# A transformer block on one core: transposing the second LayerNorm and b1 on TensorE, a shorter query ring for a fourth ffn1 weight slot, and an earlier second output projection

## The chip, the core and the metric

The kernel runs on one core of a Trainium2 chip. The core has five engines with a queue each: TensorE (PE; its weight loads are shown as PEld), VectorE (DVE), ScalarE (ACT), GpSimd (POOL) and SyncE (SP), which here issues every DMA. An engine takes its instructions in order; a wait at the head of its queue holds everything behind it. The metric is the device time of one execution in microseconds (us). Lower is better.

## What is computed

A pre-LayerNorm transformer block over 2048 tokens of width 1024, in bf16: attention with 32 heads of 32, then a feed-forward layer of width 3584 with tanh GELU, each added to its input.

```python
def _A_ref(x, wqkv, wo):                    # H = 32, Dh = 32
    qkv = (x @ wqkv).reshape(B, S, 3, H, Dh).transpose(2, 0, 3, 1, 4)
    q, k, v = qkv[0], qkv[1], qkv[2]
    p = _softmax(jnp.einsum("bhqd,bhkd->bhqk", q, k) * Dh ** -0.5, axis=-1)
    o = jnp.einsum("bhqk,bhkd->bhqd", p, v)
    return o.transpose(0, 2, 1, 3).reshape(B, S, D) @ wo

def _B_ref(x, w1, b1, w2, b2):
    return jnp.einsum("bsf,fd->bsd", _gelu(jnp.einsum("bsd,df->bsf", x, w1) + b1), w2) + b2

h  = x + _A_ref(_layernorm(x), A_wqkv, A_wo)
h2 = h + _B_ref(_layernorm(h), B_w1, B_b1, B_w2, B_b2)
```

## The kernel before

**How the order comes about.** The program does not write its instruction streams out by hand. It builds a graph of tasks (`gr.add`, line 87), each with an engine, an assumed duration, a priority and the buffers it reads and writes, and then `schedule` (line 112) simulates the five engines with these assumed durations and fixes the order of each engine's queue. `assign` (line 209) turns the dependences into semaphore waits. On the chip the order is fixed: where a DMA lands later than the planner assumed (`dma_lat=2.0` and 260 GB/s), the engine waits in place. For PE, `pick_pe` (line 1007) takes score matmuls first, then the value matmuls, then "background" groups in the order in which they were made; a group that isn't ready may be passed by a later one that is. PSUM has eight banks: six hold scores, and the remaining two are shared by one attention accumulator and the background groups, so a background group keeps a bank from its first matmul until DVE has copied it out.

**Stages.** In the lead (lines 857 to 888) x arrives in 16 tiles of 128 tokens; each is normalised by DVE and transposed (four tiles on PE with a copy by ACT, twelve by DMA transposes) into `xnT`, and the first group of four heads gets its keys, queries and values. Then attention goes by jobs `(g, c)`: eight groups g of four heads, eight chunks c of 256 queries, eight rounds a job. A round is 8 score matmuls (L682), two exponentials on ACT of 128x1024 (L690), a sum of two key blocks on DVE (`PS`, L695), 8 value matmuls (L700) and 4 matmuls with ones for the denominator (L719). The first two chunks of each group run while later groups are projected (line 933).

Behind the attention of chunk c run, as background groups, the output projection of chunk c-1 (`wo`, line 767, four groups; result plus x into `hch`), the second LayerNorm (`ln2`, line 781, two tiles of 128 tokens), `ffn1` of chunk c-1 (14 blocks of 256 columns) and `ffn2` of chunk c-2 (four groups `F2` of 29 matmuls). `PLAN` (line 952) gives how the four ffn2 groups and the ffn1 blocks alternate. GELU (line 811) is done for every two ffn1 blocks: square and polynomial on DVE into `a_sq`, tanh on ACT into `a_th`, product on DVE. After the last attention comes the tail (line 974): wo, LayerNorm, ffn1 and ffn2 of the last chunk with nothing beside them, and the tail's LayerNorm is transposed on PE with a copy by ACT.

**What the change touches.**
- `ln2_tile` (line 773): LayerNorm of one tile into the single slot of `R1.xb`, then with "dma" one DMA transpose (`dma_t`, line 522) into `hnT`. The other branch makes a background group of eight PE transposes of 128x128 (`transposes`, line 571) with one copy of the bank to `hnT` by ACT or DVE.
- b1 (lines 912 and 914): 3584 biases loaded so that partition p holds the elements p, p+128, ..., and cast to float by DVE at the lowest priority. They are read first by ffn1 (L804).
- Queries: chunks 0 and 1 are projected right into `QT`; chunks 2 to 7 are projected after the last group (`spill_q`, line 643, 24 groups), written to HBM by way of `stg`, and read back by `load_q` (line 650), eight jobs ahead, into a ring of eight slots.
- `w1r`: three slots of 512 KB for the weights of wo and ffn1 (`R1.w1`); `w2r`: seven for ffn2. In the tail both rings get slots in the space of K and V.
- `layer_norm` has a branch `on_act` that no call takes (`ACT_LN` is empty).

Of the kernel before, what the change touches and what calls it, by code (L numbers as in the profile page):

```python
# [7 lines left out]
ACT = mybir.ActivationFunctionType  # L8
ALU = mybir.AluOpType
# [3 lines left out]
P = 128  # L13
# [299 lines left out]
def build_kernel(nc, A_x, A_wqkv, A_wo, B_w1, B_b1, B_w2, B_b2, out):  # L313
# [47 lines left out]
    ones32, B_ones = sb(top, "ones32", [P, 32], BF)  # L361
    two_row, B_two = sb(top, "two_row", [P, P], BF)
    b2t, B_b2t = sb(top, "b2t", [P, D], BF)
    b1b, B_b1b = sb(top, "b1b", [P, FC], BF)
    b1f, B_b1f = sb(top, "b1f", [P, FC], F32)
    cexp, B_cexp = sb(top, "cexp", [P, 16], F32)
    NLN = 8
# [4 lines left out]
    tb, B_tb = sb(top, "tb", [P, NLN, 1], BF, NLN)  # L372
    denb, B_denb = sb(top, "denb", [P, NLN, 1], BF, NLN)
    rden, B_rden = sb(top, "rden", [P, NLN, 1], F32, NLN)
    nmr, B_nmr = sb(top, "nmr", [P, NLN, 1], F32, NLN)

    kt_lo = top.cur
    KT, B_KT_ = sb(top, "KT", [P, G, S], BF, 8 * G)
# [1 line left out]
    v_lo = top.cur  # L380
    V, B_V_ = sb(top, "V", [P, G, NT, P], BF, 8 * G)
    B_V = [B_V_[8 * g:8 * g + 8] for g in range(G)]
    NQ = 8
    QT, B_QT = sb(top, "QT", [P, NQ, 256], BF, NQ)
    pt_lo = top.cur
    NPT = 7
# [34 lines left out]
    def ring(area, name, n, width, dtype):  # L421
        h, b = sb(area, name, [P, n, width], dtype, n)
        if n == 1:
            b = [b]
        return [(h[:, i, :], b[i]) for i in range(n)]
# [2 lines left out]
        pass  # L428

    R1 = Set()  # L430
    NW1, NW2 = 3, 7
    w1r, B_w1r = sb(ffn, "w1r", [P, NW1, 2048], BF, NW1)
    hch, B_hch_ = sb(ffn, "hch", [P, 2, 2, D], BF, 8)
    B_hch = [B_hch_[:4], B_hch_[4:]]
# [2 lines left out]
    R1.xb = Ring(ring(Area(x_lo), "xb2", 1, D, BF))  # L437
    LN2_PRIO = -2
    hnT, B_hnT = sb(ffn, "hnT", [P, 2, DC, P], BF, 2)
    R1.sq = Ring(ring(ffn, "a_sq", 2, 1024, BF))  # L440
    th_lo = ffn.cur
    R1.th = Ring(ring(ffn, "a_th", 1, 1024, F32))
    stg = Ring(ring(Area(th_lo), "stg", 2, 512, BF))
    R1.os = Ring(ring(ffn, "a_os", 2, 512, BF))
    gT, B_gT_ = sb(ffn, "gT", [P, 2, FC, 256], BF, 2 * FC)
    B_gT = [B_gT_[:FC], B_gT_[FC:]]
# [13 lines left out]
    def c_dve_ps(n):  # L460
        return (120 + n) / 960.0 + 0.02
# [73 lines left out]

    cnt = {"ln": 0}

    def layer_norm(tiles, prio, on_act=False):
        n = len(tiles)
        while cnt["ln"] % NLN + n > NLN:  # L540
            cnt["ln"] += 1
        i = cnt["ln"] % NLN
        cnt["ln"] += n
        for k, (x_ap, B_x, o_ap, B_o) in enumerate(tiles):
            for c in range(2):
                dve(lambda v, c=c, k=k, x_ap=x_ap: v.bn_stats(st_l[:, i + k, 6 * c:6 * c + 6], x_ap[:, 512 * c:512 * c + 512]),  # L546
                    0.68, reads=[B_x[c % len(B_x)]], writes=[B_stl[i + k]], prio=prio)
            dve(lambda v, k=k: v.bn_aggr(mv_l[:, i + k, :], st_l[:, i + k, :]), 0.2,
                reads=[B_stl[i + k]], writes=[B_mv[i + k]], prio=prio)
        sl = slice(i, i + n)  # L550
        dve(lambda v: v.tensor_copy(mvb[:, sl, :], mv_l[:, sl, :]), 0.12, reads=B_mv[sl], writes=B_mvb[sl], prio=prio)
        dve(lambda v: v.tensor_scalar(tb[:, sl, :], mvb[:, sl, 1:2], EPS_BF, None, ALU.add), 0.12,
            reads=B_mvb[sl], writes=B_tb[sl], prio=prio)
        pool(lambda g: g.tensor_tensor(denb[:, sl, 0], tb[:, sl, 0], cexp[:, 0:n], ALU.pow), 0.42 + 0.157 * n,
             reads=B_tb[sl] + [B_cexp], writes=B_denb[sl], prio=prio)
        dve(lambda v: v.tensor_copy(mvr[:, sl, :], mvb[:, sl, 0:1]), 0.12, reads=B_mvb[sl], writes=B_mvr[sl], prio=prio)
        dve(lambda v: v.reciprocal(rden[:, sl, :], denb[:, sl, :]), 0.12, reads=B_denb[sl], writes=B_rden[sl], prio=prio)
        if on_act:
            dve(lambda v: v.scalar_tensor_tensor(nmr[:, sl, :], mvr[:, sl, :], -1.0, rden[:, sl, :], ALU.mult, ALU.mult), 0.12,
                reads=B_mvr[sl] + B_rden[sl], writes=B_nmr[sl], prio=prio)  # L560
        for k, (x_ap, B_x, o_ap, B_o) in enumerate(tiles):
            if on_act:
                act(lambda a, k=k, x_ap=x_ap, o_ap=o_ap: a.activation(
                    o_ap, x_ap, ACT.Identity, bias=nmr[:, i + k, :], scale=rden[:, i + k, :]), 1024,
                    reads=B_x + [B_nmr[i + k], B_rden[i + k]], writes=[B_o], prio=prio, ap_bias=True)
                continue
            dve(lambda e, k=k, x_ap=x_ap, o_ap=o_ap: e.tensor_scalar(
                o_ap, x_ap, mvr[:, i + k, :], rden[:, i + k, :], ALU.subtract, ALU.mult), 0.58,
                reads=B_x + [B_mvr[i + k], B_rden[i + k]], writes=[B_o], prio=prio)
# [25 lines left out]
    def x_slot(tt):  # L595
        return xrb[:, tt % NXR, :], [B_xrb[tt % NXR]]

    def x_tile(tt, prio):
        ap, b = x_slot(tt)
        return dma(ap, x2[tt * P:(tt + 1) * P, :], P * D * 2, writes=b, prio=prio)  # L600

    def ln_tiles(tts, prio, on_act=False):
        layer_norm([x_slot(tt) + (xb[:, tt % NXB, :], B_xb[tt % NXB]) for tt in tts], prio, on_act)

    def tr_tile(tt, evac):
        if evac != "dma":
# [31 lines left out]
                 [grp.buf], [B_V[2 * q][tt // 2], B_V[2 * q + 1][tt // 2]])  # L638

    def slot_of(g, c):  # L640
        return (2 * g + c) % 8 if c < 2 else g

    def spill_q(g, h):
        grp = group(f"s{g}.{h}")
# [136 lines left out]
    def ln2(R, c, evac):  # L781
        for t in range(2):
            ln2_tile(R, c, t, evac)
# [64 lines left out]
    def mixed(R, c1, c2, plan):  # L848
        blk = 0
        for p in plan:  # L850
# [3 lines left out]
            else:  # L854
                ffn2(R, c2, *p)

    x_tile(0, -6)
    x_tile(1, -6)
    load_w(WK, -6, 0, P)
# [9 lines left out]
    jobs = [Job(0, 0, 6, True), Job(0, 1, 5, True)]  # L869
    trs = []  # L870
    FULL = True
    ACT_LN, ACT_T = (), (0, 1)
    for i in range(8):
        tts = [2 * i, 2 * i + 1]
        ln_tiles(tts, 0, i in ACT_LN)
        for tt in tts:
            trs.append(tr_tile(tt, "act" if i in ACT_T else "dma"))
            if tt + NXR < NT:
                last_x = [x_tile(tt + NXR, -4)]
        proj_k(group("lead", FULL), 0, 256 * i, 256, "act")  # L880
        if i < 2:
            proj_q(group("lead", FULL), 0, 256 * i, 256, i, "dve")
        proj_v(group("lead", FULL), 2 * i, 0, "act")
        jobs[0].round()
        if i == 1:
            jobs[1].round()
        if i >= 1:
            jobs[1].round()
# [20 lines left out]
        rest_w(WK + 1, c * P, c * P + P)  # L909
        rest_w(WQ + 1, c * P, c * P + P)  # L910
    rest_w(WV + 1, 256, 512)
    dma(b1b[:], B_b1.rearrange("(fc p) -> p fc", p=P), P * FC * 2, writes=[B_b1b], noncontig=True, prio=1, after=lx)
    dma(b2t[0:1, :], B_b2.rearrange("(o d) -> o d", o=1), D * 2, writes=[B_b2t], prio=1, after=lx)
    dve(lambda v: v.tensor_copy(b1f[:], b1b[:]), 0.2, reads=[B_b1b], writes=[B_b1f], prio=3)

    n_lead = len(groups)
    B_ps[4].r += [t for grp in groups for t in grp.buf.r]
# [15 lines left out]
    for g in range(1, G):  # L933
        projections(g)
        attend(g, 0)
        attend(g, 1)

    wo(R1, 0)
    ln2(R1, 0, "dma")
    for h in range(3):  # L940
        for g in range(G):
            spill_q(g, h)
            if h == 0:
                load_q(g, 2)

    def attention(c):
        for g in range(G):
            attend(g, c)
            if c + 1 < NC:
                load_q(g, c + 1)  # L950

    PLAN = [F2[0], 4, F2[1], 5, F2[2], 5, F2[3]]
    ffn1(R1, 0, range(FC // 2))
    for c in range(2, NC):
        wo(R1, c - 1)
        ln2(R1, c - 1, "dma")
        mixed(R1, c - 1, c - 2, PLAN)
        attention(c)
    L = NC - 1
# [10 lines left out]
    R2.xb = Ring(ring(Area(kt_lo), "xbl", 2, D, BF))  # L970
    k = R1.w1.k % NW1
    R2.w1 = Ring(slots[2:12] + R1.w1.slots[k:] + R1.w1.slots[:k])
    R2.w2 = Ring(slots[12:] + R1.w2.slots)
    ws = [wo_w(R2, j) for j in range(2)]
    for t in range(2):
        for j in range(2):
# [168 lines left out]
```

## Time and profile before

| | us |
|---|---|
| four runs | 1142.89, 1140.92, 1143.47, 1138.8 |
| their median | 1141.91 |
| the profiled execution | 1142.89 |
| its span, first to last instruction | 1141.1 |
| exponentials (L690), 1024 of them, busy | 964.3 |
| landing of the b1 load (7 KB) / of one DMA transpose to hnT, median | 8.7 / 6.4 |
| landing of a w1r / w2r block of 512 KB, median | 4.4 / 6.4 |

A row of a group reads: line, engine, operation, output <- input, shape, count | busy time, mean duration in ns | idle time of the engine right before it, and what ended that idle time. Lines of helpers serve several callers: L496 and L499 are all background matmuls (L496 in four column tiles, L499 at full width), L517 all plain DMAs, L573 all PE transposes, L586 all copies of projections, so they are told apart by the names of the tiles. A timeline row reads: start, duration, engine, line, operation, count, and in brackets the idle time before it. The granted PE clock is 0.986 on average over the run.

### The profile page before, as it was taken

What the parts mean: (1) busy time and instruction counts of PE and PEld (TensorE: products, weight loads), DVE (VectorE), ACT (ScalarE), POOL (GpSimd) and SP (SyncE); (2) the same over time, 40 slices, a digit from 0 to 9 for tenths busy, and PEclk for the clock granted to TensorE, in tenths of its full rate; (3) what the DMA queues carried; (4) which work ended last, traced back from release to release, by engine and by line L of the source; (5) the groups of instructions that cost most, each with busy time, mean ns of one, the idle gap of its engine ahead of it and who ended that gap; (6) DMA issues with size and microseconds to landing.
All of it is one profiled execution on the core that took longest, in us unless ns stands there. A gap on an engine that the chain in (4) does not pass through costs nothing.

```text
span 1141.1 us, 53247 instructions
## 1 busy us (share of the span) xinstructions
PE 1070.2 (94%) x24802; PEld 608.3 (53%) x24807; DVE 817.2 (72%) x1456; ACT 1037.2 (91%) x1131; POOL 19.1 (2%) x36
## 2 busy tenths in 40 slices
PE   8989999999998999899999989999999999889998
PEld 6636464654445645654654555456446544464483
DVE  7436666666767886886897688679668957687652
ACT  4869999999998999999999989999999999999551
POOL 1000000000000000000000000000000000000000
PEclk9989999999999999999999999999999999899999
DMA  6960100003424557587556747755685757676533
GB/s 185 195 158 3 49 3 3 4 26 92 107 92 133 159 127 200 146 256 194 149 172 203 212 132 241 177 170 162 200 213 147 219 187 219 191 206 207 183 113 111
DMA packets 266478, 169.63 MB, mean 149 GB/s; under 512 B 54289, under 2 KB 264209, under 8 KB 266258
## 3 DMA queue, kind: packets, MB, share of 16 engines
q1 hardware_dynamic: 266258, 166.24, 51.4%
q8 instruction: 194, 3.18, 1.2%
q14 instruction: 26, 0.21, 0.1%
HBM read 152.05 MB, written 7.34 MB: 140 GB/s over the span
## 4 chain that ended last, share of the span: by engine, by line
PE 70%; ACT 18%; DVE 5%; issue 2%; SPq 2%; DMA 2%; POOL 0%; DVEq 0%; POOLq 0%
PE ps L496 41%; ACT PT L690 17%; PE ps L682 11%; PE ps L700 7%; PE ps L499 6%; PE ps L719 4%; SPq L517 2%; DVE gT L804 1%; ACT a_th L822 1%; PE ps L867 1%; DMA b1b<-in_B_b_dram 1%; DVE PS L695 1%; DVE st L546 1%; DMA w1r<-in_B_w_dram 0%; DVE stg L586 0%
## 5 line engine op out<-in xcount | busy, mean ns | idle before, releaser
L690 ACT ACTIVATE PT<-ps 128x1024 bf16<-128x1024 f32 x1024 | 964.3, 1037 | 38.5 <-PE ps L682 34.7
L695 DVE TENSOR_TENSOR PS<-PT 128x1024 bf16<-128x1024 bf16 x496 | 329.7, 683 | 98.3 <-ACT PT L690 50.9
L496 PE MATMUL ps<-hnT,w1r 128*32 128x256 bf16 x6272 | 222.7, 276 | 21.0 <-DVE gT L804 10.1
L682 PE MATMUL ps<-QT,KT 32*128 32x256 bf16 x4096 | 205.5, 275 | 10.3 <-ACT PT L690 8.5
L496 PE MATMUL ps<-w2r,gT 128*32 128x512 bf16 x3076 | 212.7, 381 | 1.3 <-issue 0.8
L700 PE MATMUL ps<-PT,V 128*32 128x256 bf16 x4096 | 189.6, 276 | 8.8 <-ACT PT L690 6.6
L496 PEld LDWEIGHTS ps<-hnT,w1r 128*32 128x32 bf16 x6272 | 159.2, 97 | 62.5 <-issue 49.3
L682 PEld LDWEIGHTS ps<-QT,KT 32*128 32x128 bf16 x4096 | 61.1, 92 | 167.9 <-ACT PT L690 119.2
L719 PE MATMUL ps<-PS,ones 128*32 128x256 bf16 x1984 | 144.5, 277 | 2.7 <-issue 1.4
L496 PE MATMUL ps<-xnT,Wall 128*32 128x512 bf16 x1888 | 130.9, 385 | 10.5 <-DVE KT L586 6.7
L700 PEld LDWEIGHTS ps<-PT,V 128*32 128x32 bf16 x4096 | 101.0, 97 | 58.3 <-ACT PT L690 20.8
L496 PEld LDWEIGHTS ps<-w2r,gT 128*32 128x32 bf16 x3076 | 72.9, 96 | 66.3 <-issue 24.9
L804 DVE TENSOR_TENSOR gT<-ps,b1f 128x512 bf16<-128x512 f32 x98 | 67.2, 686 | 28.5 <-PE ps L496 27.0
L719 PEld LDWEIGHTS ps<-PS,ones 128*32 128x32 bf16 x1984 | 54.0, 96 | 40.6 <-DVE PS L695 25.5
L496 PEld LDWEIGHTS ps<-xnT,Wall 128*32 128x32 bf16 x1888 | 44.3, 97 | 51.4 <-issue 21.7
L823 DVE SCALAR_TENSOR_TENSOR gT<-a_th,gT 128x1024 bf16<-128x1024 f32 x49 | 59.6, 1216 | 3.6 <-ACT a_th L822 3.6
L496 PE MATMUL ps<-w1r,OT 128*32 128x512 bf16 x896 | 58.8, 381 | 1.9 <-DVE hch L764 0.9
L820 DVE SCALAR_TENSOR_TENSOR a_sq<-a_sq,gT 128x1024 bf16<-128x1024 bf16 x49 | 59.7, 1219 | 0.6
L496 PE MATMUL ps<-Wall,xnT 128*32 128x256 bf16 x1536 | 51.3, 273 | 1.8 <-DVE V L586 1.3
L822 ACT ACTIVATE a_th<-a_sq 128x1024 f32<-128x1024 bf16 x49 | 52.4, 1069 | 0.5 <-DVE a_sq L820 0.4
L728 DVE STREAM_TRANSPOSE DT<-ps 128x256 f32<-128x256 f32 x64 | 28.6, 447 | 24.2 <-PE ps L719 24.1
L496 PEld LDWEIGHTS ps<-Wall,xnT 128*32 128x32 bf16 x1536 | 38.1, 96 | 10.1 <-issue 6.6
(80 smaller groups left out, 609.3 us busy)
## 6 DMA issues: line engine op xcount, KB each, us to landing
w2r<-in_B_w_dram SPq DMA_DIRECT2D x108, 512.0 KB, 6.4
w1r<-in_B_w_dram SPq DMA_DIRECT2D x101, 512.0 KB, 4.4
w1r<-in_A_wo_dram SPq DMA_DIRECT2D x28, 512.0 KB, 4.1
xrb<-in_A_x_dram SPq DMA_DIRECT2D x16, 256.0 KB, 4.1
Wall<-in_A_wqkv_dram SPq DMA_DIRECT2D x16, 256.0 KB, 5.4
wk<-in_B_w_dram SPq DMA_DIRECT2D x8, 512.0 KB, 4.6
a_x<-in_A_x_dram SPq DMA_DIRECT2D x28, 128.0 KB, 4.5
out_dram<-a_os SPq DMA_DIRECT2D x28, 128.0 KB, 5.5
```

The source lines that it names most:

```text
L496: fns.append(lambda p, j=j: p.matmul(dst(32 * j, 32 * j + 32), lhsT[:, 32 * j:32 * j + 32], rhs, start=start, stop=stop, tile_position=(0, ...
L499: t.alt = [lambda p: p.matmul(dst(0, P), lhsT, rhs, start=start, stop=stop, skip_group_check=True)]
L682: fns.append(lambda p, i=i, hh=hh, r0=r0: p.matmul(psum[:, 2 * us[hh // 2] + hh % 2, 256 * i:256 * i + 256], KT[r0:r0 + 32, g, 256 * r + P ...
L690: act(lambda a, u=u, q=q: a.activation(PT[:, s, 2 * q:2 * q + 2, :], psum[:, 2 * u:2 * u + 2, :], ACT.Exp, bias=0.0, scale=SCALE), 1024, r ...
L695: dve(lambda v: v.tensor_tensor(PS[:, z, :, :], PT[:, s, :, 0:256], PT[:, s, :, 256:512], ALU.add), c_dve(1024, 2), reads=B_PT[s], writes= ...
L700: fns.append(lambda p, i=i, hh=hh: p.matmul(psum[32 * hh:32 * hh + 32, self.bank, 0:256], V[:, g, 2 * r + i, 32 * hh:32 * hh + 32], PT[:, ...
L719: fns.append(lambda p, i=i, hh=hh, src=src: p.matmul(psum[32 * hh:32 * hh + 32, self.bank, 256:512], ones32[:, :], src[:, hh, :], start=False,
L728: dve(lambda v: v.transpose(DT[:, f, :], psum[:, self.bank, 256:512]), c_dve_ps(256), reads=[self.buf], writes=[B_DT[f]], prio=-1)
L804: gate[c] = dve(lambda v, xh=xh, fc=fc, grp=grp: v.tensor_tensor(xh, psum[:, grp.bank, :].rearrange("p (f n) -> p f n", f=2), b1f[:, fc:fc ...
L820: dve(lambda v: v.scalar_tensor_tensor(v4(sq), v4(sq), C2, xh, ALU.add, ALU.mult), c_dve(n), reads=[b_sq] + b_xh, writes=[b_sq], prio=1)
L822: act(lambda a: a.activation(th, sq, ACT.Tanh, bias=0.0, scale=K2 / 2), n, reads=[b_sq], writes=[b_th], prio=-1, kind="tanh")
L823: t = dve(lambda v: v.scalar_tensor_tensor(xh, v4(th), 1.0, xh, ALU.add, ALU.mult), c_dve(n), reads=[b_th] + b_xh, writes=b_xh, prio=1)
```

## The change

The second LayerNorm of chunks 0 to 6 goes through PE transposes and a DVE copy. b1 is loaded in 28 rows of 128 elements and transposed by one PE transpose in a group made just before the first wo. The query ring has four slots and is refilled four jobs ahead; the space gives `w1r` a fourth slot, and `a_sq` goes from two slots to one. The second wo is made before ffn1 of chunk 0 instead of after it; its LayerNorm stays behind that ffn1. The plan has ffn1 blocks 2, 5, 5, 2 between and after the ffn2 groups instead of 4, 5, 5. In the tail the ffn2 ring gets five more slots. The unused `on_act` branch and its tile `nmr` go.

```diff
-    b1b, B_b1b = sb(top, "b1b", [P, FC], BF)
+    b1b, B_b1b = sb(top, "b1b", [FC, P], BF)
-    nmr, B_nmr = sb(top, "nmr", [P, NLN, 1], F32, NLN)
-    NQ = 8
+    NQ = 4
-    NW1, NW2 = 3, 7
+    NW1, NW2 = 4, 7
-    R1.sq = Ring(ring(ffn, "a_sq", 2, 1024, BF))
-    th_lo = ffn.cur
+    sq_lo = ffn.cur
+    R1.sq = Ring(ring(ffn, "a_sq", 1, 1024, BF))
     R1.th = Ring(ring(ffn, "a_th", 1, 1024, F32))
-    stg = Ring(ring(Area(th_lo), "stg", 2, 512, BF))
+    stg = Ring(ring(Area(sq_lo), "stg", 2, 512, BF))
...
     def slot_of(g, c):
-        return (2 * g + c) % 8 if c < 2 else g
+        return (2 * g + c) % NQ if c < 2 else g % NQ
...
+    def b1_on_partitions():
+        grp = group("b1")
+        grp_pe(grp, lambda p: p.transpose(psb[:, grp.bank, 0:FC], b1b[:], ident[0:FC, 0:FC]), 0.064, [B_b1b, B_ident], "full")
+        dve(lambda v: v.tensor_copy(b1f[:], psb[:, grp.bank, 0:FC]), c_dve_ps(FC), reads=[grp.buf], writes=[B_b1f])
...
-    dma(b1b[:], B_b1.rearrange("(fc p) -> p fc", p=P), P * FC * 2, writes=[B_b1b], noncontig=True, prio=1, after=lx)
+    dma(b1b[:], B_b1.rearrange("(fc p) -> fc p", p=P), P * FC * 2, writes=[B_b1b], prio=1, after=lx)
     dma(b2t[0:1, :], B_b2.rearrange("(o d) -> o d", o=1), D * 2, writes=[B_b2t], prio=1, after=lx)
-    dve(lambda v: v.tensor_copy(b1f[:], b1b[:]), 0.2, reads=[B_b1b], writes=[B_b1f], prio=3)
...
+    b1_on_partitions()
     wo(R1, 0)
-    ln2(R1, 0, "dma")
+    ln2(R1, 0, "dve")
     for h in range(3):
         for g in range(G):
             spill_q(g, h)
-            if h == 0:
+            if h == 0 and g < NQ:
                 load_q(g, 2)
...
     def attention(c):
         for g in range(G):
             attend(g, c)
-            if c + 1 < NC:
-                load_q(g, c + 1)
+            c2, g2 = divmod(G * c + g + NQ, G)
+            if c2 < NC:
+                load_q(g2, c2)

-    PLAN = [F2[0], 4, F2[1], 5, F2[2], 5, F2[3]]
+    PLAN = [F2[0], 2, F2[1], 5, F2[2], 5, F2[3], 2]
+    wo(R1, 1)
     ffn1(R1, 0, range(FC // 2))
     for c in range(2, NC):
-        wo(R1, c - 1)
-        ln2(R1, c - 1, "dma")
+        if c > 2:
+            wo(R1, c - 1)
+        ln2(R1, c - 1, "dve")
         mixed(R1, c - 1, c - 2, PLAN)
         attention(c)
...
-    R2.w2 = Ring(slots[12:] + R1.w2.slots)
+    R2.w2 = Ring(slots[12:] + R1.w2.slots + slots[6:11])
```

More of the change, by code (lines that the diff above doesn't have):

```diff
@@ L536, in build_kernel, with layer_norm @@
     cnt = {"ln": 0}
-    def layer_norm(tiles, prio, on_act=False):
+    def layer_norm(tiles, prio):
         n = len(tiles)
@@ L557, in layer_norm @@
         dve(lambda v: v.reciprocal(rden[:, sl, :], denb[:, sl, :]), 0.12, reads=B_denb[sl], writes=B_rden[sl], prio=prio)
-        if on_act:
-            dve(lambda v: v.scalar_tensor_tensor(nmr[:, sl, :], mvr[:, sl, :], -1.0, rden[:, sl, :], ALU.mult, ALU.mult), 0.12,
-                reads=B_mvr[sl] + B_rden[sl], writes=B_nmr[sl], prio=prio)
         for k, (x_ap, B_x, o_ap, B_o) in enumerate(tiles):
[L562 to L566, printed above, removed]
             dve(lambda e, k=k, x_ap=x_ap, o_ap=o_ap: e.tensor_scalar(
@@ L600, in x_tile, with ln_tiles @@
         return dma(ap, x2[tt * P:(tt + 1) * P, :], P * D * 2, writes=b, prio=prio)
-    def ln_tiles(tts, prio, on_act=False):
-        layer_norm([x_slot(tt) + (xb[:, tt % NXB, :], B_xb[tt % NXB]) for tt in tts], prio, on_act)
+    def ln_tiles(tts, prio):
+        layer_norm([x_slot(tt) + (xb[:, tt % NXB, :], B_xb[tt % NXB]) for tt in tts], prio)
     def tr_tile(tt, evac):
@@ L871, in build_kernel @@
     FULL = True
-    ACT_LN, ACT_T = (), (0, 1)
+    ACT_T = (0, 1)
     for i in range(8):
         tts = [2 * i, 2 * i + 1]
-        ln_tiles(tts, 0, i in ACT_LN)
+        ln_tiles(tts, 0)
         for tt in tts:
```

## The prediction

> **What bounds the kernel now.** I read the page first, for the shares of each engine and its costliest groups.
>
> ```profile
> PE 1070.2 (94%) x24802; PEld 608.3 (53%) x24807; DVE 817.2 (72%) x1456; ACT 1037.2 (91%) x1131; POOL 19.1 (2%) x36
> ...
> L690 ACT ACTIVATE PT<-ps 128x1024 bf16<-128x1024 f32 x1024 | 964.3, 1037 | 38.5 <-PE ps L682 34.7
> ```
>
> PE has the largest share, but the shares are averages over three stages. So next the windows, cut at the places where ACT starts and stops being full.
>
> ```profile
> 82.00:354.00 272.00, 260.47 (x6412) 140.51 (x6412) 181.50 (x335) 269.64 (x289) 1.11 (x2) 1.00 0.17 46
> 354.00:1071.00 717.00, 674.46 (x16996) 383.91 (x16992) 559.61 (x953) 694.73 (x743) 9.35 (x12) 0.99 0.64 184
> 1071.00:1141.00 70.00, 64.22 (x438) 39.76 (x435) 34.66 (x52) 20.90 (x38) 1.09 (x2) 0.97 0.44 137
> ```
>
> The columns are span, then PE, PEld, DVE, ACT, POOL busy, clock and DMA. Between 82 and 1071 us ACT is busy 964.4 of 989, so its exponentials set the pace, and in those 989 us only ACT's own idle time can be won: the waits of ACT there add up to 21.4 (on L682, the scores) + 0.6 + 0.4 = 22.4 us. PE idles 42.5 us in 354:1071; background matmuls (projections, wo, ffn) may take that without moving the end. Before 82 and after 1071 PE and the loads decide.
>
> The third view is the timeline around the largest hole, DVE first, then PE, then ACT.
>
> ```profile
> 75.80 0.18 DVE L914 CAST b1f<-b1b 128x28 f32<-128x28 bf16 x1 [6.42 <-DMA b1b<-in_B_b_dram]
> ...
> 77.32 1.04 PE L496 MATMUL ps<-xnT,Wall 128*32 128x512 bf16 x8 [4.71 <-DVE KT L586]
> ...
> 78.96 1.94 ACT L690 ACTIVATE PT<-ps 128x1024 bf16<-128x1024 f32 x2 [5.37 <-PE ps L682]
> 82.61 33.67 ACT L690 ACTIVATE PT<-ps 128x1024 bf16<-128x1024 f32 x36 [1.72 <-PE ps L682]
> ```
>
> DVE stands at the b1 cast from 69.4 to 75.8 although nobody needs b1 before 338. Behind it in DVE's queue are the PS sum and the KT evacuation; PE waits for that bank, and ACT for PE. After 82.6 ACT runs 33.67 us without a gap and from there to 354 idles 2.4 us, so what is lost here is kept to the end.
>
> The fourth view is the second LayerNorm of the last chunk that goes by DMA (DVE, SP, SP, DVE, then PE's next background matmul).
>
> ```profile
> 964.69 0.55 DVE L567 TENSOR_SCALAR xb<-hch,mvr,rden 128x1024 bf16<-128x1024 bf16 x1
> 966.49 3.30 SPq L523 DMA_TRANSPOSE hnT<-xb  x1
> ...
> 977.14 0.54 DVE L567 TENSOR_SCALAR xb<-hch,mvr,rden 128x1024 bf16<-128x1024 bf16 x1
> ...
> 977.71 1.24 SPq L523 DMA_TRANSPOSE hnT<-xb  x1
> ...
> 982.67 1.28 PE L496 MATMUL ps<-hnT,w1r 128*32 128x256 bf16 x20
> ```
>
> The one xb slot makes the second tile wait until the first transpose has landed (966.5 + 6 to 8 us). From 963.7+1.25 to 982.7 PE gets no background matmul; ACT stays full, but the backlog is paid in 984:1034, where ACT idles 50.00 - 45.87 = 4.13 us.
>
> **The change, part by part**, against the profiled execution: 1142.89 us, span 1141.1, so 1.8 outside. The runs' median, 1141.91, is 1.0 lower.
>
> *b1.* The load of 3584 single elements becomes 28 rows; the cast leaves DVE's early queue; one PE transpose and one small DVE copy (the cast's 0.18) are queued after the last projection, near 250 us, long after the load has landed, and before 338. Gain: ACT's two gaps 5.37 + 1.72 = 7.09, less one ordinary gap of this place (0.67 to 0.89, at 65 and 68 us) = 6.3. Bounds: 0 if the wait only moves, 8.6 if every ACT wait of 64 to 84 us goes. Take -6.3. [...]
>
> *Second LayerNorm, 14 tiles.* Removed: 14 DMA transposes (issue 1.24 to 4.17 us of SP, 6.4 median to landing). SP's time is nobody's; DVE's waits for them are 2.2 us in three places; take -0.5 (0 to -2.2). The hole at 965: tile two would now wait for 0.61 us of transposes (the tail's row for eight) and a copy, some 3 us a tile, so about 12 of 17 us of hole go. Half of the 4.13 us: take -2.0 (0 to -4.1).
>
> Added: 112 transposes, 14 x 0.61 = 8.5 us, with two changes of tile shape at 0.21 each (the gap before L682's loads): 14 x 1.03 = 14.4 us of PE. DVE copies 128x1024 out of PSUM: no such row; 256 columns take 0.389 and 512 take 0.686, which extended gives 1.28; from below, 0.68 (L695, SBUF). I take 1.28 as it is PSUM: 17.9 us of DVE. Cover: PE's 42.5 us idle and ACT-bound windows; DVE is busy 67% in the seven stretches around these tiles. If the cover is gone, a tile costs 0.61 + 0.42 + 1.28 = 2.31 us, 32 us in all, since background groups have one bank at a time and stop until DVE has copied. What I charge: five of these stretches (410:440, 520:545, 618:650, 718:750, 828:858) show ACT idle of 0.91 + 0.37 + 0.28 + 0.34 + 0.24 = 2.14 us for ten tiles; as much again for fourteen: +3.0 (0 to +32).
>
> [...] The tail's rows say 219 ns each but overlapped, 0.61 for eight, so I keep 0.61.
>
> *Shorter query ring.* Same 48 reloads, four jobs (some 60 us) ahead instead of eight; landing takes 2.2 us median, 7.3 at most. In the projections a group's queries must wait for the group two before it: the QT casts stand at 121.8, 138.6, 180.3, 197.2, 237.7 and the jobs they would overwrite write OT at 107.1, 139.2, 169.3, 199.9, 229.8. A job's last scores come some 7 us before its OT, so all are free. Zero; if a slot were late, a few us each.
>
> *One a_sq slot.* L819 must wait for the tanh before it. Of the 43 I read, five start under 4 us after the one before (750.4 to 754.2 is one); the rest have room. +0.5 (0 to 5 x 3 = +15).
>
> *Fourth w1 slot, plan, wo(1) forward, more w2 slots in the tail.* Waits for w1r loads are 0.2 us in the whole trace, for w2r in the tail 1.0. Moving wo(1), four groups with their loads of weights and a_x past the ffn1 loads in SP's queue, changes the order of background work, not its amount. Together -0.5 (-1.2 to 0). PE's stalls at "issue" (9.8 us on L496, 1.80 at 362.9 and 2.62 at 672.7) come after 21 and 7 matmuls of a run, inside a task of four, where no wait stands; I leave them, though a new order moves them, which is 3 us of noise either way.
>
> Sum: -6.3 - 0.5 - 2.0 + 3.0 + 0.5 - 0.5 = -5.8, so 1137.1 by the profile, 1136 by the median.
>
> **Rivals.**
> 1. *Larger gain:* steadier weights and early LayerNorm also halve ACT's 22.4 us: -7.1 - 11.2 - 1.0 = -19.3, 1123. For it: ACT idle sits in ffn1 stretches (362 to 400, 984 to 1034). Against: the largest gaps there follow "issue" stalls, which nothing here touches.
> 2. *The b1 wait moves or is eaten:* PE stops at the b1 transpose, or ACT takes the added work in small pieces: -6.3 + 6 = 1142. Against: b1's group comes after all projections.
> 3. *Slower:* the background bank. Each tile holds it through 0.61 us of PE and DVE's 1.28 behind whatever DVE has queued (two PS sums, 1.4); ffn1 starts later and ACT runs dry in the ffn1 stretch, where DVE is 93 to 98% busy. Full price 14 x (2.31 + 1.4) = 52; half of it, 26, less 8.8: +17, 1159. It decides from 8.8 / 14 = 0.63 us of ACT idle per tile. For it: ACT already waits for PE 21.4 us; against: the stretches of the tiles show 0.21 us a tile and PE has 42.5 us.
> 4. *The fourth slot does nothing:* it is in my sum already, as 0.2 us of waits.
>
> **How the numbers follow.** Forecast (1125 to 1138.5) 0.57, larger gain 0.13, moved or eaten 0.13, slower 0.17. One measurement tells 0.3%, 3.4 us, from no change: faster 0.70, same 0.13, slower 0.17. The likeliest is 1136. The sum's own range is 1125 to 1143 (low: 8.6 + 4.1 + 2.2 + 1.2 with no cost; high: b1 gains nothing and the tiles cost little). To leave out no more than 2 in 10 with the +32 end open, it goes to 1122 on one side and 1148 on the other.
>
> **What would show it.** Right: DVE without a wait for b1b; ACT with no gap over 1 us from 66 to 90; ACT idle in the middle stage near 22; the background hole at the last LayerNorm under 6 us; PE transposes 0.6 us for eight. Wrong: ACT idle in the stretches of the tiles above 0.6 us each, PE waiting for an hnT copy by DVE, scores that wait for a QT load, or an ACT gap of 5 us at b1's new place.

## The result, and the profile after

The changed kernel takes 1144.38 us (median of 43 runs, 1137.77 to 1150.22) beside 1141.53 for the kernel before (64 runs, 1135.49 to 1149.12): ratio 1.0024, interval 1.0012 to 1.0035. It is a little slower; 1136 and a gain were forecast. The profiled execution took 1144.6, its span is 1142.5. Two later traces (e9 and e20) are of disturbed executions of 1698 and 2542 us; they are not read, and these two times do not enter the medians of e9 and e20.

The page of the changed kernel: busy time of each engine, the row of the exponentials, and the queue that the page calls instruction (packets, MB, share).

```profile
PE 1071.7 (94%) x24909; PEld 611.8 (54%) x24914; DVE 824.3 (72%) x1470; ACT 1036.6 (91%) x1131; POOL 17.3 (2%) x36
...
q8 instruction: 195, 3.19, 1.2%
...
L681 ACT ACTIVATE PT<-ps 128x1024 bf16<-128x1024 f32 x1024 | 964.5, 1038 | 44.8 <-PE ps L673 40.0
```

PE and DVE have 1.5 and 7.1 us more work than before, and ACT stood 44.8 us ahead of its exponentials, where it had stood 38.5. Next the windows, cut as before (span, then PE, PEld, DVE, ACT, POOL busy, clock, DMA share, GB/s).

```profile
82.00:354.00 272.00, 261.29 (x6311) 138.47 (x6314) 184.48 (x353) 270.02 (x290) 2.80 (x4) 1.00 0.15 45
354.00:1071.00 717.00, 668.02 (x16896) 384.83 (x16888) 553.48 (x933) 681.04 (x729) 5.84 (x10) 0.99 0.60 180
1071.00:1142.00 71.00, 66.97 (x544) 41.64 (x537) 38.18 (x58) 25.04 (x43) 1.09 (x2) 1.00 0.43 130
```

Up to 354 us nothing is lost. In the long stage ACT is busy 681.0 of 717, before it was 694.7: 13.7 us went there. Ahead of that stage the change had won. ACT's timeline where the b1 hole was:

```profile
62.92 1.94 ACT L681 ACTIVATE PT<-ps 128x1024 bf16<-128x1024 f32 x2 [0.67 <-PE ps L673]
65.75 41.00 ACT L681 ACTIVATE PT<-ps 128x1024 bf16<-128x1024 f32 x44 [0.89 <-PE ps L673]
```

After 65.75 it runs 41 us without a gap; job (1,0) writes OT, its result, at 82.5 us, 9.5 earlier than before (2.2 of that it already had at the first job). The last job's OT comes at 1078.5, 4.0 later than before. So some 13.5 us were lost between. What PE waited for between 354 and 1060 us, the view of waits, first before, then after (engine, tile, line, what it waited for: us, times, longest; "issue" is idle time for which the profile shows no wait). The last line of each is ACT's own.

```profile
PE ps L496 <- DVE gT L804: 11.9, 23, 1.0
PE ps L496 <- issue: 9.8, 12, 2.6
...
PE ps L700 <- issue: 1.1, 2, 0.8
PE ps L719 <- issue: 1.1, 2, 0.7
...
PE ps L682 <- issue: 1.0, 1, 1.0
...
ACT PT L690 <- PE ps L682: 19.5, 30, 3.1
```

```profile
PE ps L495 <- issue: 19.0, 18, 2.5
PE ps L673 <- ACT PT L681: 8.7, 17, 1.2
PE ps L495 <- DVE gT L795: 7.8, 18, 1.0
...
PE ps L710 <- issue: 2.5, 2, 1.7
PE ps L673 <- issue: 2.3, 2, 1.7
...
PE ps L691 <- issue: 0.5, 1, 0.5
...
ACT PT L681 <- PE ps L673: 32.8, 32, 2.6
```

All "issue" rows together grew from 13.0 to 24.3 us, the waits for DVE fell from 18.5 to 9.8, and ACT's own waits grew from 19.9 to 32.8. One such stall on PE's timeline, and ACT's answer:

```profile
448.10 1.17 PE L495 MATMUL ps<-hnT,w1r 128*32 128x256 bf16 x36
450.93 0.62 PE L495 MATMUL ps<-hnT,w1r 128*32 128x256 bf16 x16 [1.66 <-issue]
451.48 0.40 PE L673 MATMUL ps<-QT,KT 32*128 32x256 bf16 x8
```

```profile
439.56 10.60 ACT L681 ACTIVATE PT<-ps 128x1024 bf16<-128x1024 f32 x11
451.93 3.77 ACT L681 ACTIVATE PT<-ps 128x1024 bf16<-128x1024 f32 x4 [1.76 <-PE ps L673]
```

PE stops in the middle of a group; the profile shows no wait; the next scores come late, and ACT loses 1.76 us. What stalls of this kind are is to be read from the instruction queue. Its 195 packets are of 16,384 bytes each (3.19 MB in all), and PE's 49,823 instructions (24,909 matmuls and 24,914 weight loads) divided by 195 are 255.5 a packet, 64 bytes for one. By this count, an estimate from the page, a packet is a page of some 256 PE instructions. From one stall to the next PE loads weights 128, 254, 508 or 1273 times, and so on: multiples of 127.4 loads in the changed kernel and of 127.6 in the kernel before, half a page's instructions. So all these stalls stand whole pages apart, at page ends by the same estimate. In each the packet that had come last had landed only 1.3 to 1.7 us before PE went on; for the other pages it had lain there 2.4 us before and 2.7 after, at the median. Such packets took no longer than the rest (median 1.05 us before and 1.12 after, the rest 1.07 and 1.05), so it was their start that was late, as far as two traces tell. In the 2.5 us ahead of that start the DMA engines were busy 64% or more in every case (median 77% before, 98% after; ahead of the other packets 77% and 72%); of the 58 packets of the two traces that started after less than 50% none stalled PE.

```
stalls of PE at issue over 0.2 us, 354 to 1060 us     before        after
pages / stalled / idle in them, us                    132/17/13.0   131/22/24.1
```

**Theory A:** weight traffic delays PE's instruction fetches, and an edit that moves tasks or page ends (the second half is called D in the last expectations) draws a new set of delays. Its rivals: density, PE using up pages faster than they can be fetched, whatever else moves (B in the next expectation); the change's work and order cost of themselves (transposes on PE, an early wo, rings; C in the later expectations), or one part alone does, such as the fourth w1 slot, whose loads run further ahead. The granted clock is no rival: it was 0.994 in the changed kernel's traced execution and 0.986 before.

### The profile page after: what moved, and what is told of

The parts are those of the page before. It is cut to its first block, busy times and chain, and to the rows that moved or that the text cites. A ratio compares the mean times of both kernels' runs of the same rounds, so it can differ in the third digit from the quotient of the medians.

```text
span 1142.5 us, 53460 instructions
## 1 busy us (share of the span) xinstructions
PE 1071.7 (94%) x24909; PEld 611.8 (54%) x24914; DVE 824.3 (72%) x1470; ACT 1036.6 (91%) x1131; POOL 17.3 (2%) x36
## 3 DMA queue, kind: packets, MB, share of 16 engines
q8 instruction: 195, 3.19, 1.2%
## 4 chain that ended last, share of the span: by engine, by line
PE 68%; ACT 23%; DVE 5%; issue 3%; POOL 0%; DVEq 0%; POOLq 0%
PE ps L495 38%; ACT PT L681 22%; PE ps L673 11%; PE ps L498 7%; PE ps L691 7%; PE ps L710 4%; DVE gT L795 1%; DVE PS L686 1%; ACT a_th L813 1%; PE ps L863 1%; DVE a_sq L811 1%; PE ps L564 0%; DVE gT L814 0%; DVE KT L577 0%; DVE V L577 0%
## 5 line engine op out<-in xcount | busy, mean ns | idle before, releaser
L681 ACT ACTIVATE PT<-ps 128x1024 bf16<-128x1024 f32 x1024 | 964.5, 1038 | 44.8 <-PE ps L673 40.0
L691 PE MATMUL ps<-PT,V 128*32 128x256 bf16 x4096 | 186.5, 274 | 5.9 <-ACT PT L681 4.4
L495 PE MATMUL ps<-xnT,Wall 128*32 128x512 bf16 x1888 | 128.3, 381 | 5.4 <-DVE KT L577 1.9
L691 PEld LDWEIGHTS ps<-PT,V 128*32 128x32 bf16 x4096 | 101.8, 96 | 49.0 <-ACT PT L681 13.8
L814 DVE SCALAR_TENSOR_TENSOR gT<-a_th,gT 128x1024 bf16<-128x1024 f32 x49 | 59.7, 1219 | 14.3 <-ACT a_th L813 14.3
```

Source lines behind the costliest of these rows:

```text
L495: fns.append(lambda p, j=j: p.matmul(dst(32 * j, 32 * j + 32), lhsT[:, 32 * j:32 * j + 32], rhs, start=start, stop=stop, tile_position=(0, ...
L681: act(lambda a, u=u, q=q: a.activation(PT[:, s, 2 * q:2 * q + 2, :], psum[:, 2 * u:2 * u + 2, :], ACT.Exp, bias=0.0, scale=SCALE), 1024, r ...
L691: fns.append(lambda p, i=i, hh=hh: p.matmul(psum[32 * hh:32 * hh + 32, self.bank, 0:256], V[:, g, 2 * r + i, 32 * hh:32 * hh + 32], PT[:, ...
L814: t = dve(lambda v: v.scalar_tensor_tensor(xh, v4(th), 1.0, xh, ALU.add, ALU.mult), c_dve(n), reads=[b_th] + b_xh, writes=b_xh, prio=1)
```

## The experiments

Ratios are to the kernel before in the same session (medians 1138.3 to 1140.7 us). "Issue" is PE's idle time at issue between 354 and 1060 us, always of the kernel's one traced execution.

**The same order with less traffic (e1).**

```diff
+        k = DC if not b.w or b.w[0].eng != E.SP else 2
-        dma(w, src_ap.rearrange("(dc p) c -> p dc c", p=P), P * 4096, writes=[b], prio=1, after=lx)
+        dma(w[:, 0:k], src_ap.rearrange("(dc p) c -> p dc c", p=P)[:, 0:k], P * 4096, writes=[b], prio=1, after=lx)
```

(and the like for w2, one of four blocks)

> The changed kernel with every instruction and every order as it is, but each load of ffn and wo weights after the first one into a slot brings only the first quarter of its block (the rest of the slot keeps older weights, so the feed-forward part and wo are computed with stale weights). Theory A, traffic: the weight loads delay the fetches of PE's instructions. Then the waits at issue on PE in 354:1071, 24.3 us in the changed kernel, fall under 12, ACT's waits there from 32.9 to 22 or less, and the time by 10 us or more, ratio to before about 0.992 or less. Theory B, density: PE uses up a page of 256 instructions faster than pages can be fetched, whatever else moves. Then the issue waits stay above 20 and the time within 3 us of 1144 (ratio 1.000 to 1.005). Theory C, the rival of the prediction (bank held through DVE's copies): as B for the time, but with ACT idle next to the LayerNorm tiles.

1114.5 us, ratio 0.9786 (0.9759 to 0.9813). Issue fell from 24.3 to 1.6 us, ACT's waits for scores from 32.8 to 5.5, and PE's waits for DVE stayed (9.8, 10.4). The stalls hang on the traffic, and density alone (B) is out.

**b1 alone (e2), three w1 slots (e3), old order (e4).** In e2 only b1's load, transpose and cast are changed; e3 has `NW1, NW2 = 3, 7`; e4 has

```diff
-    PLAN = [F2[0], 2, F2[1], 5, F2[2], 5, F2[3], 2]
-    wo(R1, 1)
+    PLAN = [F2[0], 4, F2[1], 5, F2[2], 5, F2[3]]
...
-        if c > 2:
-            wo(R1, c - 1)
+        wo(R1, c - 1)
```

> The kernel before with the b1 part of the change alone. If the 9.5 us that the changed kernel is ahead at 92 us come from b1 and the rest of the change loses them: about 1133, ratio 0.992, ACT waits in 354:1071 near the 19.9 of before. If any new order of the tasks costs as much by itself (a rival): ratio 0.998 to 1.003, ACT waits in the middle near 30.

> The changed kernel with three w1 slots. If the fourth slot is what bunches the weight loads (theory A with the slot as its cause): issue waits on PE in the middle near 13, ratio 0.993. If not: issue waits above 20, ratio 1.000 to 1.005.

> The changed kernel with the plan (4, 5, 5) and the place of the second wo as before. If the hole of background work at 407 to 425 (second wo moved forward) and the ffn1 blocks at the end of the plan cost the middle stage: 4 to 10 us faster than the changed kernel, ratio 0.994 to 0.999, and no background hole near 415. If fetches or bank are the cause wherever ffn1 stands: ratio 1.000 to 1.005.

e2: 1129.99 us, ratio 0.9913 (0.9883 to 0.9943), issue 7.6. e3: 1143.42, 1.0041 (1.0020 to 1.0062): by its time the fourth slot is not the cause. Its trace says less: issue is 13.8, as expected if the slot were the cause, in a quick execution (1139.6) whose last OT comes at 1065.3 and is followed by 72.3 us, in the changed kernel by 64.0. e4: 1134.13, 0.9965 (0.9947 to 0.9984), issue 9.6. At this point the list of tasks and the early wo looked guilty of half of the loss. The later runs took that back.

**A new base (e9, e13).** From here on the first LayerNorm's last 12 tiles are transposed on PE as well, so that no kernel of the set has a DMA transpose:

```diff
-            trs.append(tr_tile(tt, "act" if i in ACT_T else "dma"))
+            trs.append(tr_tile(tt, "act" if i in ACT_T else "dve"))
```

> The changed kernel with one edit in its lead, which this and all later kernels share: the last 12 tiles of the first LayerNorm are transposed by PE and copied back by VectorE too, in place of a DMA transpose each. It is the base that they are compared with. The lead (to about 66 us) gains 96 transposes on PE (12 tiles at about 0.6 us for eight, so 7 us) and 12 copies of 0.684 us, part of them hidden behind the loads of x: the kernel should be 0 to 8 us behind the changed kernel (ratio to the kernel before 1.002 to 1.010), and from 354 to 1060 us its background work is the same list of tasks. Theory A: PE's idle time at issue there stays high (18 us or more). If it falls below 12 us with the same list of tasks, the list is not what decides, only where the fetches happen to fall.

> The base of the set again (the changed kernel with all of the first LayerNorm transposed on PE): its trace was taken at a granted clock of 0.556 and can't be read beside the others. By the traces of the others the lead now costs 8.8 us more (first OT of job (0,0) at 71.3 us, not 62.5), so with the changed kernel's middle it should stand at 1150 to 1153 us; it stood at 1145.9. Theory A, with fetches that fall anew in each kernel: PE's idle time at issue between 354 and 1060 us is 4 to 8 us below the changed kernel's 24.3, with the same list of tasks. Rival (the early second wo and the list cost the same wherever the fetches fall): idle time at issue 22 to 26 us again, and the 5 us come from elsewhere, ScalarE's tail or PE's waits behind VectorE.

1145.77 us, 1.0072 (1.0045 to 1.0098), and again 1147.82, 1.0083 (1.0057 to 1.0109); e13 gives the trace. The first OT comes at 70.4 us, 7.9 late, and by the ratios the kernel is 5.5 to 6.7 us behind the changed one, so one or two of the 7.9 us are made up. Issue is 22.7, where the rival had it and not theory A, and ACT's waits between 354 and 1060 us are 28.3, 4.5 below the changed kernel's. This pair settles nothing, it only sets the base.

**The order edits one by one and together (e10, e14, e19).** Each as in e4's diff.

> The base of this set (the changed kernel with all of the first LayerNorm transposed on PE) with the second wo put back to its old place, behind ffn1 of chunk 0; the new list of background tasks stays. If the second wo's early place is what costs (the stretch from 407 to 425 us in which PE had 2 of 10 us free and ScalarE waited 0.93, 0.43 and 1.40 us): 5 to 9 us ahead of the base. If the list of tasks is what costs: within 2 us of the base. If neither alone, and each new order draws its own set of late fetches: anything between, and the time follows PE's idle time at issue between 354 and 1060 us, about 1 us per us (24.3 in the changed kernel, 9.6 with both orders put back).

> The base of the set with the old list of background tasks; the second wo stays in its new place. If the list costs: 5 to 12 us ahead of the base (1134 to 1141 beside 1145.9). If it needs both edits undone, or neither decides: within 2 us of the base, as with the second wo put back alone (1145.8). The time follows PE's idle time at issue: 18.9 us between 354 and 1060 with the second wo put back, 9.2 with everything but b1 and the LayerNorm as before.

> The base of the set with both the old list of tasks and the old place of the second wo; new rings, four w1 slots and one a_sq slot stay. One at a time they gave 0 to 3 us of the 12 to 14 us that lie between the base (1147) and the old kernel with b1 and LayerNorm (1133.6). If the two together make up the order's cost: 1132 to 1137 us, ratio 0.994 to 0.999. If the rings and the a_sq slot hold the rest: 1139 to 1143 us, ratio 1.000 to 1.004. Theory A expects PE's idle time at issue between 354 and 1060 us to go with the time: near 9 us in the first case, 12 to 16 in the second.

Old wo: 1145.75, 1.0060 (1.0037 to 1.0083), issue 18.9. Old list: 1144.25, 1.0052 (1.0031 to 1.0074), issue 11.0 in a quick execution (1138.6). Both: 1145.59, 1.0066 (1.0039 to 1.0094), issue 17.4. Undoing both gains nothing here, where it had gained 0.6% in e4: the same edit, another result. An edit with a fixed price of its own does not do that.

**b1 and LayerNorm in the old order and rings (e11).**

> The kernel before with two of the change's parts, b1 from contiguous rows and the second LayerNorm transposed on PE, and the first LayerNorm wholly on PE as in the base of this set. Two slots of a_sq, three w1 slots, eight slots of the query ring, the old list of tasks and the old place of the second wo. Theory A (only the order of the background work costs): 10 to 15 us ahead of the base, as b1 alone was of the changed kernel (ratios 0.9913 and 1.0024 to 1.0041), PE's idle time at issue between 354 and 1060 us at 7 to 11 us. Rival C (the 112 transposes and 28 copies of the second LayerNorm are added work on a PE that is 94% busy, at about 0.4 us a tile): 4 to 9 us ahead of the base, as with both orders put back (0.9965), with PE's idle time behind VectorE above the 17.5 us of b1 alone.

1133.59 us, 0.9960 (0.9940 to 0.9979): 12 to 14 us ahead of the base. Issue is 9.2, PE's waits for DVE are 21.7, ACT's waits 14.3. Theory A's number, with C's sign in the waits for DVE; these cost ACT little.

**Fewer instructions (e12, e15).** ffn1 at full width in the old and in the new order:

```diff
-            grp = group(f"f1.{c}.{blk}")
+            grp = group(f"f1.{c}.{blk}", True)
```

> The kernel of the entry before (b1 and both LayerNorms on PE, old order) with the matmuls of ffn1 on the whole array (128x128 weights) in place of four quarters of 128x32: a quarter as many matmuls and weight loads in ffn1, so some 9400 of 49,800 PE instructions fewer, and the same rows streamed. Theory A: fewer instructions mean fewer fetches (some 37 of 195 pages fewer) and less idle time at issue (below 7 us between 354 and 1060): 2 to 10 us ahead of the kernel with quarters, unless changing between whole and quarter array costs more than that: by the planner's 0.21 us per change and two changes for each of some 128 groups it could cost as much as 54 us where no slack takes it up. Rival (fetches are a by-product and PE's own work sets the pace): within 2 us of the kernel with quarters.

> The base of the set with ffn1 on the whole array: some 9400 PE instructions fewer in 49,800, the changed kernel's order and rings as they are. Theory A (the order costs only through late fetches, so with few of them it costs nothing): the gain over the base is two to four times the 3.2 us that the same edit brought in the old order, 8 to 14 us, to 1132 to 1138 us beside 1130.4, and PE's idle time at issue between 354 and 1060 us falls below 6 us. Rival (the order costs through work and waits of its own: early wo, fewer query slots, one a_sq slot): the gain is the same 2 to 5 us as in the old order, 1141 to 1144 us, with PE's idle time at issue as low.

Old order: 1130.39, 0.9925 (0.9903 to 0.9948), 3.2 us ahead of e11; issue 1.8. New order: 1128.89, 0.9916 (0.9890 to 0.9942), 17 to 19 us ahead of the base, more than either side expected; issue 1.0. The page of the latter:

```profile
PE 1088.9 (97%) x20147; PEld 593.7 (53%) x20153; DVE 832.2 (74%) x1482; ACT 1035.2 (92%) x1131; POOL 17.9 (2%) x36
...
q8 instruction: 158, 2.59, 1.0%
```

158 pages in place of 196, the DMA share of the long stage as high as before (0.61), and the two orders are level. Its PE and ACT waits there:

```profile
PE ps L672 <- ACT PT L680: 4.7, 12, 0.5
...
PE ps L495 <- issue: 0.8, 1, 0.8
```

```profile
ACT PT L680 <- PE ps L672: 1.2, 4, 0.6
```

ACT now hardly ever waits: attention runs at its pace (last OT at 1054.4 us), and background work that found no room follows after it (73.4 us from there to the end, 64.0 in the changed kernel). The edit is not a pure change of fetches: PE's waits for DVE fall too (21.7 to 8.5 in the old order).

**The LayerNorm twice (e16).**

```diff
             transposes(group(f"t{c}.{t}"), o, bo, hnT[:, t, :, :], B_hnT[t], evac)
+            transposes(group(f"u{c}.{t}"), o, bo, hnT[:, t, :, :], B_hnT[t], evac)
```

> The kernel with b1 and both LayerNorms on PE in the old order (1133.6 us), with every transposition of the second LayerNorm done twice, the second time over the first with the same result: another 112 transposes on PE (14 tiles at about 0.62 us, 8.7 us) and 14 copies by VectorE (0.684 us each, 9.6 us) between 354 and 1060 us and in the tail. Rival C (each tile stalls ScalarE by some 0.4 us): 5 to 7 us behind. Theory A (PE's work there fits into its slack, and the fetches decide): 0 to 3 us behind, and which way is set by PE's idle time at issue, 9.2 us without the doubling.

1150.65 us, 1.0114 (1.0088 to 1.0140), 17 us behind e11. Both expectations missed. The attention isn't later (last OT at 1066.0, in e11 1068.8; issue 9.5 and 9.2), but the time from there to the end is 83.1 us in place of 64.6. PE's ffn2 matmuls at full width after the last OT, in e11 and in this kernel (tile row: count, shortest/median/longest ns, first to last start):

```profile
L498 PE MATMUL ps<-w2r,gT x100: 376/379/380, 1074.1 to 1129.7; 128*128 128x512 bf16 x100
```

```profile
L498 PE MATMUL ps<-w2r,gT x176: 376/379/389, 1071.2 to 1145.8; 128*128 128x512 bf16 x176
```

76 more matmuls of ffn2 were left for the tail, where PE is busy 78.9 us after the last OT, in e11 60.7; that the extra transposes, 8.7 us of PE, crowded them out by the time for which they hold a bank is likely but not shown. By these two traces background work beside this attention is nearly at its limit: what was added came back after it.

**Both orders with the traffic cut (e17, e18).** The edit of e1.

> The base of the set (the changed kernel, first LayerNorm on PE) with loads of w1, w2 and wo cut: after a slot's first load each one brings only the first quarter of the tile, so the weights used are partly those of an earlier tile; the instructions of the compute engines and their order are the base's. It is run for the pair with the next entry. Theory A: some 25 us ahead of the base (1147 us), as the changed kernel's cut version was ahead of it (1114.5 beside 1144), plus the longer lead: 1117 to 1124 us, and within 3 us of the old order with cut loads. Rival C (early wo, four query slots, one a_sq slot cost of themselves): 4 to 12 us behind the old order with cut loads.

> The other half of the pair: b1 and both LayerNorms on PE, old order and rings, loads of w1, w2 and wo cut to the first quarter in the same way. Uncut the two stand 12 to 14 us apart (1133.6 and 1146 to 1148). Theory A (the order costs only by where weight loads meet the instruction fetches): within 3 us of the entry before, 1115 to 1122 us. Rival C: 4 to 12 us ahead of it, 1107 to 1115 us.

New order 1120.85 us, 0.9840 (0.9816 to 0.9863); old order 1122.56, 0.9846 (0.9822 to 0.9870). Uncut they are 12 to 14 us apart, cut they are level. The window of the long stage in the new order, first the base (e13), then with cut loads: DMA share 0.23 in place of 0.60, ACT busy 692.0 of 706 in place of 674.3.

```profile
354.00:1060.00 706.00, 658.76 (x16716) 381.08 (x16708) 549.77 (x936) 674.26 (x721) 7.42 (x11) 0.99 0.60 179
...
354.00:1060.00 706.00, 676.62 (x17174) 389.29 (x17167) 566.79 (x974) 692.03 (x742) 7.96 (x11) 1.00 0.23 67
```

Rival C's price for order and rings is not there, at least while the loads are cut.

**Page ends moved, nothing else (e20, e21, e22).** In the first microseconds, 16 or 32 of the 80 warm-up matmuls are split in three:

```diff
+    def warm3(p):
+        for a, b in ((0, 84), (84, 168)):
+            p.matmul(psum[:, 6, a:b], ident[:, :], b2t[:, a:b], start=True, stop=True)
+        return p.matmul(psum[:, 6, 168:256], ident[:, :], b2t[:, 168:256], start=True, stop=True)
-        pe(lambda p: p.matmul(psum[:, 6, 0:256], ident[:, :], b2t[:, 0:256], start=True, stop=True), 0.12,
+        pe(warm3 if k < 32 else lambda p: p.matmul(psum[:, 6, 0:256], ident[:, :], b2t[:, 0:256], start=True, stop=True), 0.12,
```

> The base of the set (1145.9 and 1147.8 us) with 16 of the 80 warm-up matmuls ahead of the first tile each split into three narrower ones (84, 84 and 88 columns in place of 256): 64 PE instructions more in the first 10 us, a quarter of a page of 256, and from there on every instruction in the same order, with the same traffic. All later page ends fall 64 instructions earlier in the work. Theory D (where the page ends fall among the weight loads decides): the time moves by 2 us or more, either way, within 1134 to 1152 us, and goes with PE's idle time at issue between 354 and 1060 us (22.7 in the base). Rival (an edit of the change costs of itself, through the traffic's order or the rings): within 2 us of the base, idle time at issue 21 to 25 us.

> The same with 32 of the warm-up matmuls split in three: page ends half a page earlier. Theory D: 1134 to 1152 us, not the same as the base nor as the shift by a quarter, by 2 us or more from at least one of them. Rival: within 2 us of the base.

> The kernel with b1 and both LayerNorms on PE in the old order (1133.6 us, PE's idle time at issue 9.2 us between 354 and 1060) with the same half-page shift. Theory D: the old order's small idle time is in part a lucky place of its page ends, so it goes up: 1136 to 1146 us, idle time at issue 11 to 20 us. Rival (the old order is better of itself): within 2 us of 1133.6.

New order: 1145.73, 1.0063 (1.0039 to 1.0087) at a quarter page; 1145.95, 1.0070 (1.0041 to 1.0099) at half a page, issue 22.1: no more than 2.1 us from either run of the base, not what theory D expected. Old order: 1148.69, 1.0082 (1.0057 to 1.0108), from 1133.59 with, by the two traces, the same instructions in the same order on every engine after the warm-up, and the same traffic. 15.1 us by 128 more PE instructions (64 matmuls and their weight loads) in the first microseconds, more than the 1136 to 1146 that theory D expected. The runs do not overlap (1132.15 to 1138.87, 12 runs; 1141.98 to 1151.1, 6 runs), the first OT is only 0.8 us later, and the clock was 1.000 and 0.999. Its waits at issue beside those of e11, first e11:

```profile
PE ps L495 <- issue: 8.0, 9, 1.5
PE ps L698 <- issue: 0.9, 2, 0.7
PE ps L680 <- issue: 0.3, 1, 0.3
```

```profile
PE ps L495 <- issue: 7.3, 8, 1.6
PE ps L698 <- issue: 4.1, 3, 2.2
PE ps L680 <- issue: 2.2, 4, 1.2
PE ps L717 <- issue: 1.2, 2, 1.1
```

As many stalls as before fall on background matmuls; those on scores (L680), values (L698) and denominators (L717) go from 1.2 to 7.5 us, and ACT's waits for scores from 13.9 to 18.1. The trace shows under half of the 15.1 us: it is of e22's quickest run, 6.7 us behind e11's traced one, with 5.6 us more issue. That the rest has the same cause is not shown by a trace.

Seven kernels of the set with full loads and quarter-width ffn1 give one table, each by its one profiled execution, with the median of all its runs beside it:

```
                      issue us   time us   median us
e11 old order            9.2     1135.2      1133.6
e14 old list            11.0     1138.6      1144.3
e22 old order, shifted  14.8     1142.0      1148.7
e19 both orders old     17.4     1143.3      1145.6
e10 old wo              18.9     1146.5      1145.8
e21 new order, shifted  22.1     1151.5      1146.0
e13 new order           22.7     1149.9      1147.8
```

A straight line through the first two columns is 1125.4 + 1.12 x issue, with no point more than 1.5 us off; 13.5 us more of idle time at issue (e13 beside e11) are 14.7 us more of time. The line ties an execution's idle time to its own time. It does not rank the kernels: six of the seven have medians between 1144.3 and 1148.7, though their traces show 11.0 to 22.7. Left out is e16, which has more work and lies 15 us above the line. The kernels with DMA transposes have a lead that is some 8 us shorter; with 7.9 us taken off, b1 alone lies 2 us below the line, the changed kernel on it, e4 and e3 5 and 7 us above it. So issue is a large term here and not the only one.

## Why the prediction was wrong, point by point

- *b1, -6.3:* right in mechanism and nearly in size. The cast, ahead of which DVE stood for 6.4 us, leaves its queue, the transpose comes at 241.0 us without a wait, and the lead over the kernel before is 9.5 us at job (1,0), 7.3 of it won in the hole. b1 alone brought 0.87% (8 us by the medians, 10 by the ratio), part of it perhaps luck: its issue was 7.6.
- *Second LayerNorm, DVE copies at 1.28 us:* mis-sized. The 14 copies of 128x1024 out of PSUM took 0.684 us each, 9.6 us of DVE and not 17.9. The lower bound of the copy, 0.68, was the right one. Around the last LayerNorm (960 to 981 us) no gap between PE's background matmuls is over 2 us, so the hole at 965 closed as forecast. Net price: e11 lies 0.0047 behind b1 alone, and its longer lead is worth 0.0054 (e17 against e1), which leaves about nothing. That is an estimate over four kernels that carries their draws: with e22 in e11's place it would be 1.15%. e16 shows that as much again does not fit.
- *Query ring and a_sq, 0 and +0.5:* right by the trace: no wait for a QT load among PE's, none for a_sq among ACT's in the long stage.
- *Fourth slot:* right (e3).
- *The plan and wo(1), "changes the order of background work, not its amount", together -0.5:* the amount was indeed the same, but here the sum failed, with the sentence after it: the issue stalls "I leave them, though a new order moves them, which is 3 us of noise either way". They were 13.0 us in the long stage; they became 24.3, and ACT's waits grew by 12.9 with them. By the fitted line the 11.3 us are worth 12.7, an estimate, which eats b1's gain of 9.5 and makes the 3 us that the result shows. So the step that failed is the stalls' zero in the sum, with 3 us of noise around it: they moved by 11.3. Nor was the cover free, PE's 42.5 us of idle time: 13.0 of them were these stalls and 18.5 waits for DVE. It isn't the new order as such: with cut loads or with ffn1 at full width both orders are level, and the old order with page ends half a page off (e22) is as slow.
- *Rival 1's objection*, that the gaps follow issue stalls "which nothing here touches": the gaps do follow them, and an edit that moves an instruction or a load can move them, as e22 shows. *Rival 3* (the bank held for DVE) did not come: PE's waits for DVE fell. *Rival 2* named the outcome, a gain that is eaten, but not by what.
- The range needed a term from the trace: 17 of 132 pages stalled, up to 2.6 us each, 13.0 us in all. With none or twice as many, an estimate, it is -13 to +13 us; the runs here went from 1.0 to 24.3.

Open: whether the new order stalls more on average over all places of its page ends (three places gave 1145.7 to 1147.8 us) than the old one (two gave 1133.6 and 1148.7). Why a shift moves the old order and not the new one is not known, nor why kernels with nearly the same median have such different idle times in their traces; one trace a kernel is too few for that.

## What to carry to other kernels

Where PE is nearly full and loads are heavy (here PE 94% busy, DMA at 0.60 in the long stage), read "issue" waits as a term of their own: count the pages of the instruction queue, see which ends stall, and put the sum into the range of the forecast, since an edit elsewhere may move it (by 15 us of time in e22, by next to nothing in e20 and e21). A comparison of two small edits then needs each of them at several page positions; otherwise it may rank the draws. What lowered the term in both orders, from 22.7 us in the new and 9.2 in the old, was fewer PE instructions (full-width groups, 1.0 and 1.8 us) or less traffic beside them (2.0 and 1.0 us): ffn1 at full width made the changed kernel, even with its longer lead, 0.84% quicker than the kernel before (ratio 0.9916, 0.9890 to 0.9942); b1 alone gave as much (0.9913), with a draw in it.

## What the hardware showed that was not expected

- One half-page shift of PE's instruction stream moved 1133.59 us to 1148.69 in one order; in the other a quarter and a half page moved the time by no more than 2.1 us.
- The spread from run to run may have the same cause, which is not shown. It is 13.6 us over 64 runs of the kernel before and 12.5 over 43 of the changed one. Over six runs it is 1.1 us with ffn1 at full width in the new order (e15) but 4.1 in the old (e12), 1.6 to 3.9 with cut loads (e1, e17, e18), and 4.0 to 9.1 in five kernels without either.
- Most page ends cost nothing. Of the 131 packets in the long stage of the changed kernel, 109 went without a stall over 0.2 us; the other 22 cost PE 24.1 us. With small traffic the idle time at issue there was 1.0 and 2.0 us in all (e18 and e17), with fewer instructions 1.0 and 1.8 us (e15 and e12).
